# Attention and a channel MLP on one core: both heads of a pair read by one instruction where their PSUM banks lie side by side

## The chip, the core and the metric

The program runs on one core of one Trainium2 chip. A core has a matrix engine (TensorE, PE in the profile), a vector engine (VectorE, DVE), an engine for activation functions (ScalarE, ACT), a general engine (GpSimd, POOL) and a queue that issues most of the DMAs (SyncE, SP). TensorE writes its results into PSUM, which here is eight banks of 128 partitions by 512 float32; VectorE and ScalarE read them there. The metric is the device time of one execution in microseconds. The kernel before takes 2213.96 us (median of 3 runs, 2212.55 to 2215.34).

## What is computed

```python
def _A_ref(x, wqkv, wo):            # x: 1 x 2048 x 576
    H = 32; Dh = D // H             # 32 heads of 18
    qkv = (x @ wqkv).reshape(B, S, 3, H, Dh).transpose(2, 0, 3, 1, 4)
    q, k, v = qkv[0], qkv[1], qkv[2]
    p = softmax(einsum("bhqd,bhkd->bhqk", q, k) * Dh ** -0.5)
    o = einsum("bhqk,bhkd->bhqd", p, v)
    return o.transpose(0, 2, 1, 3).reshape(B, S, D) @ wo

def _B_ref(x, w1, b1, w2, b2):      # 576 -> 4608 -> 576
    h = gelu(einsum("bsd,df->bsf", layernorm(x), w1) + b1)
    return einsum("bsf,fd->bsd", h, w2) + b2

g = sigmoid((x * gate_w).sum(-1, keepdims=True))
out = g * _A_ref(x, wqkv, wo) + (1 - g) * _B_ref(x, w1, b1, w2, b2)
```

All of it is float32. Full attention over 2048 tokens with 32 heads of 18 and the MLP are independent of each other until the last line.

## The kernel before

Most matrix products take float32 operands split into a high and a low part, so that three fast products stand for one. A head has 18 columns; a query tile holds them three times (18 high, 18 high, 18 low) and a key tile to match, so one score matmul has 54 rows of depth. Heads are worked two at a time: head 0 of a pair lies on rows 0 to 63 of the array, head 1 on rows 64 to 127, and their two matmuls run side by side. Two such matmuls, one per head, are called a **pair** below.

The softmax takes two passes over the scores.

- **The maxima** (`s1_round`, L230 and L232). A pair of score matmuls, 128 queries by 512 keys for each head, goes into two banks, and VectorE reduces each bank to one maximum per query with `tensor_reduce`. This is called a max pair. After 32 rounds `s1_finish` puts the maxima into two extra rows of the query tile.
- **The exponentials** (`s2`, L275 and L278). A pair of score matmuls with 56 rows of depth (the maxima are in the product) gives 128 keys by 512 queries for each head, and ScalarE writes the exponential of each bank into a tile `p`. This is called an exp pair.
- **The product with V** (`pv`, L293). Two or three chunks of 128 keys at a time, their `p` tiles go through a burst of matmuls into one bank that collects the output of a unit (two heads, 1024 queries).

The program has 32 units of 16 chunks; a chunk has two half rounds. Each half round issues one exp pair of this unit and one max pair of a later unit (the maxima run ahead), so the two kinds alternate. 40 max pairs run before the loop, during the projection of Q, K and V. Between the pairs lie pieces of the MLP, cut to fill: `h_pair` (72 of them, 27 pairs of matmuls on 512 columns each, L494) and `out_pair` (144 of them, 24 pairs on 288 columns, L582). The readers of the MLP's banks are L514 on VectorE and L515 on ScalarE for the first, L599 on VectorE (two instructions) for the second; a Gelu chain in between goes over ScalarE and GpSimd (L547, L545, L183). The order on every engine is the order in which the code emits (`manual_schedule`); each engine takes its instructions in this order and waits at one until its semaphores are there. The weight load of a matmul is an instruction of its own (PEld in the profile), and a matmul's wait stands at its weight load.

**Banks.** A pool of PSUM tiles hands out its banks in turn, and the first matmul into a bank waits until the last reader of that bank is done. In the loop the scores have five banks, given out by `score_bank`: three of the pool `ps_s1` and then two of `ps_s2`, so bank after bank in a ring of five. A pair takes two places of the ring: the pair number k has places 2k and 2k+1, counted modulo 5. So the bank of a pair's head 0 was last used by head 1 of the pair three back, which is of the other kind, and the bank of head 1 was last used by head 0 of the pair two back, which is of the same kind. One bank holds the output of `pv` (`ps_o`), two are for the MLP (`ps_w`). Before the loop the scores have three banks and `ps_o`, and four more serve the projections.

Of the kernel before, what the change touches and what calls it, by code (L numbers as in the profile page):

```python
# [8 lines left out]
F32 = mybir.dt.float32  # L9
F32R = mybir.dt.float32r  # L10
AF = mybir.ActivationFunctionType
ALU = mybir.AluOpType
# [4 lines left out]
P = 128  # L17
# [16 lines left out]
GC0 = 1.0 / 0.044715  # L34
LN_EPS = 1e-5
HALF = S // 2
NS1 = 3
LEAD = 4
FILL = 1250.0
SLOT = 950.0  # L40
# [29 lines left out]
def gated_mix_kernel(ctx: ExitStack, tc: tile.TileContext, x, wqkv, wo, w1, b1, w2, b2, gate_w, out):  # L70
# [32 lines left out]
    pp = ctx.enter_context(tc.tile_pool(name="pp", bufs=2))  # L103
    hp = ctx.enter_context(tc.tile_pool(name="hp", bufs=6))
    asm = ctx.enter_context(tc.tile_pool(name="asm", bufs=2))
    ps_s1 = ctx.enter_context(tc.tile_pool(name="ps_s1", bufs=NS1, space=PSUM))
    ps_o = ctx.enter_context(tc.tile_pool(name="ps_o", bufs=1, space=PSUM))
    QA = [att.tile([P, HALF], F32R, name=f"qa{i}") for i in range(3)]
    KA = [att.tile([P, S], F32R, name=f"ka{i}") for i in range(2)]
    VT = [att.tile([P, NT, VW], F32, name=f"vt{i}") for i in range(2)]  # L110
# [2 lines left out]
    V0 = att.tile([P, NT, VW], F32, name="v0")  # L113
    oe = att.tile([P, TB], F32, name="oe")

    def psum(pool):
        return pool.tile([P, TB], F32, name="ps")

    ring = [0]

    def score_bank():

        ring[0] += 1
        if not looped[0]:
            return psum(ps_s1 if ring[0] % (NS1 + 1) < NS1 else ps_o)
        return psum(ps_s1 if ring[0] % (NS1 + 2) < NS1 else ps_s2)

    def big_tile():
        return yp.tile([P, 9, TB], F32R, name="big")
# [62 lines left out]
    def unit(u):  # L192
        return UNITS[u]
# [26 lines left out]
    def s1_round(u, r):  # L220


        t, kb = (r % 8, r // 8) if u in (0, NU - 3) else divmod(r, 4)
        if r == 0:
            M4[u] = asm.tile([P, 2, 8, 4], F32, name="m4")
        qa, ka = QA[u % 3], KA[unit(u)[0] % 2]
        for h in range(2):
            r0 = 64 * h
            ps = score_bank()
            nc.tensor.matmul(ps, qa[r0:r0 + 54, t * P:(t + 1) * P], ka[r0:r0 + 54, kb * TB:(kb + 1) * TB],  # L230
                             start=True, stop=True)
            nc.vector.tensor_reduce(M4[u][:, h, t, kb:kb + 1], ps, axis=AX.X, op=ALU.max)  # L232

    def s1_finish(u):

# [28 lines left out]
    def p_of(n):  # L264
        return RING[n % 4 if n < TWOS else (n - TWOS) % 3]

    def s2(u, kc, qb):
        qa, ka = QA[u % 3], KA[unit(u)[0] % 2]
        n = u * NT + kc
        if n < 2 and qb == 0:  # L270
            RING.insert(n, pp.tile([P, 2, 2, TB], F32, name="p"))
        ps = [score_bank() for _ in range(2)]
        for h in range(2):
            r0 = 64 * h
            nc.tensor.matmul(ps[h], ka[r0:r0 + 56, kc * P:(kc + 1) * P], qa[r0:r0 + 56, qb * TB:(qb + 1) * TB],  # L275
                             start=True, stop=True)
        for h in range(2):
            nc.scalar.activation(p_of(n)[:, qb, h], ps[h], AF.Exp, scale=SCALE)  # L278

    OB = {}  # L280

    def pv(n, m):

        u, kc = divmod(n, NT)
        if kc == 0:
            OB[u] = psum(ps_o)
        v = v_of(unit(u)[0])
        for c in range(n, n + m):
            for qb in range(2):
                for h in range(2):  # L290
                    r = 32 * (2 * h + qb)
                    k = c % NT
                    nc.tensor.matmul(OB[u][r:r + 32, :], v[:, k, 19 * h:19 * h + 32], p_of(c)[:, qb, h, :],  # L293
                                     start=(k == 0), stop=(k == NT - 1))
        if kc + m == NT:
            o_store(u, OB.pop(u))
# [45 lines left out]
    def mlp():  # L342
# [122 lines left out]
        def h_pair(q, last, inner=False):  # L465
# [5 lines left out]
                yield 0  # L471
            wt = ready(W1, q)
            del W1[q]
            ps = [psum(ps_w) for _ in range(2)]
# [77 lines left out]
        def out_pair(i, t, acc):  # L552

            tb, g = seq[i]
            tok = slice(t * P, (t + 1) * P)
            cs = [slice(nn * ND, (nn + 1) * ND) for nn in range(2)]
            ps = [psum(ps_w) for _ in range(2)]
            skip.clear()
            if piece[0]:
                ends = cuts(24, GAPS - piece[0]) | {12}  # L560
            elif rounds:
                ends = set(TURNS)
                skip.add(3)
            else:
                ends = set(TAIL)
                skip.update((2, 3))
            k = 0
            ends_at = []
            for turn in range(2):
                if turn == 1:  # L570
                    nc.tensor.wait_ge(swap, swaps[0])
                for j in ORDER:
                    while (i, j) not in HT:
                        cut[0] = 3
                        yield 0
                    hh, hl = HT[i, j]
                    w_ = ready(W2, (i * (G // 2) + j // 2, j % 2))
                    for h_, p_ in ((hh, 0), (hh, 1), (hl, 0)):
                        for h in (0, 1) if turn == 0 else (1, 0):
                            r = slice(64 * h, 64 * h + 64)  # L580
                            nn = h ^ turn
                            mm = nc.tensor.matmul(ps[nn][:, :ND], h_[r, tok], w_[p_][r, cs[nn]],  # L582
                                                  start=(k == 0), stop=(k == 6 * G - 1))
                            if k == 3 * G - 1:
                                ends_at.append(mm)
                        k += 1
                        if k == 3 * G:

                            seen = nc.scalar.sem_inc(swap, 1)
                            swaps[0] += 1  # L590
                            for mm in ends_at:
                                behind_of(seen, mm)
                        if k < 6 * G:
                            if k in ends:
                                cut[0] = 1
                            yield 131
            for nn in range(2):
                dst = acc[:, t, cs[nn]]
                nc.vector.scalar_tensor_tensor(dst, ps[nn][:, :ND], 0.5, b2b[:, cs[nn]] if g == 0 else dst,  # L599
                                               op0=ALU.mult, op1=ALU.add)  # L600
# [116 lines left out]
    with ExitStack() as a:  # L717
        wpool = a.enter_context(tc.tile_pool(name="a_w", bufs=1, side="right"))
        sm = a.enter_context(tc.tile_pool(name="a_sm", bufs=2, side="right"))
        ps_a = a.enter_context(tc.tile_pool(name="ps_a", bufs=4, space=PSUM))  # L720

        qkstack = ExitStack()
        wqk = qkstack.enter_context(tc.tile_pool(name="a_wqk", bufs=1))
# [41 lines left out]
                eng.tensor_tensor(lo[:, cs], raw[:, cs], hi[:, cs].bitcast(F32), op=ALU.subtract)  # L765

        def transposed(tb, c):
            ps = psum(ps_a)
# [66 lines left out]

        def stat_rows(tb):

            ps = psum(ps_a)
# [47 lines left out]
        def qk_group(tb, mt):  # L886
            big = xT[tb]
            wh, wl = W_QK
            ms = slice(mt * P, (mt + 1) * P)
            ps = psum(ps_a)  # L890
            k = 0
            for c in range(4):
                for w_, s_ in ((wh, c), (wh, 4 + c), (wl, c)):
# [12 lines left out]
        def v_group(tb, t, n, between=None):  # L906
# [4 lines left out]
            ps = psum(ps_a)  # L911
            k = 0
            for c in range(4):
                for s_, w_ in ((c, wh), (c, wl), (4 + c, wh)):
# [36 lines left out]
        for tb in range(NB):  # L951
            work = [(qk_group, (tb, mt)) for mt in (range(9) if tb < 2 else (4, 0, 1, 2, 3, 5, 6, 7, 8))] + [(v_group, (tb, t, n)) for t in range(4) for n in range(2)]
            for g, (fn, args) in enumerate(work):
# [35 lines left out]
                if tb == NB - 1:  # L989
                    if g == 0:  # L990
                        next(stream[0])
                    if g == 1:
                        load_k(0, 3 * TB, S)
                    if g == 2:
                        load_q(1)
                        next(stream[0])
                    if g == 9:
                        qkstack.close()
                        wp1 = mstack.enter_context(tc.tile_pool(name="m_w1", bufs=3))
                        wp2 = mstack.enter_context(tc.tile_pool(name="m_w2", bufs=4))  # L1000
                        next(stream[0])
                    if g == 7:
                        ps = psum(ps_a)
                        nc.tensor.transpose(ps[:, :NFC], b1r, ident[:NFC, :NFC])
                        nc.vector.tensor_copy(b1t, ps[:, :NFC])
                if tb == 1 and g == 5:
# [19 lines left out]
                    run_due()  # L1026


    ps_s2 = ctx.enter_context(tc.tile_pool(name="ps_s2", bufs=2, space=PSUM))
    ps_w = ctx.enter_context(tc.tile_pool(name="ps_w", bufs=2, space=PSUM))  # L1030
    cw = ctx.enter_context(tc.tile_pool(name="c_w", bufs=1, side="right"))
    ring2 = cw.tile([P, 2, 2, TB], F32, name="ring2")
    rstack = ExitStack()
# [7 lines left out]
    def out_proj():  # L1041
# [165 lines left out]
        for b in range(NB):  # L1207
# [6 lines left out]
            for t in range(4):  # L1214
# [5 lines left out]
                res = io.tile([P, D], F32, name="res", bufs=6)  # L1220
                for n in range(2):
                    cs = slice(n * ND, (n + 1) * ND)
                    ps = psum(ps_w)
                    k = 0
                    for c in range(5):
                        while done[b] <= c:
# [120 lines left out]
```

## Time and profile before

| | |
|---|---|
| median of 3 runs | 2213.96 us |
| profiled execution | 2212.78 us, of which the span of the instructions is 2211.0 us |
| TensorE busy | 2197.4 us (99%) |
| weight loads busy | 1578.5 us (71%) |
| VectorE busy | 1647.9 us (75%), 2888 instructions |
| ScalarE busy | 1425.9 us (64%), 2623 instructions |
| GpSimd busy | 1003.7 us (45%) |
| granted TensorE clock | 1.000 |

The times that follow are of the profiled execution. A busy TensorE is not one at its peak: the ends of matmuls are modelled, and a matmul that started late is not seen as idle time. A row of the groups gives the busy time (overlaps counted once), the mean length of one instruction, and behind the second bar the idle time of the engine before these instructions with what ended most of it. In the timeline a row is one or more like instructions in succession: start, length from the first start to the last end, engine, line, operation and count.

### The profile page before, as it was taken

The page shows a single profiled execution, that of the slowest core. Times are in us where ns is not written, and L with a number is a line of the kernel's source. Part 1 is how long each engine was busy: PE and PEld are TensorE (multiplying, and loading weights), DVE is VectorE, ACT ScalarE, POOL GpSimd, SP SyncE. Part 2 cuts the span into 40 slices and gives each one's busy share as a digit, 9 for nine tenths or more (in the row PEclk, how much of TensorE's full clock was granted, in tenths as well). Part 3 has the DMA queues.
Part 4 walks back from the last instruction along what each step waited for, and adds up shares of the span by engine and source line. Part 5 has one row for each costly group of instructions (what it writes and reads, how often), then busy time and mean ns, then how long its engine had stood idle before and what let it go on. Part 6 is the DMA issues. An engine that isn't in the chain of part 4 may idle for free.

```text
span 2211.0 us, 51479 instructions
## 1 busy us (share of the span) xinstructions
PE 2197.4 (99%) x20496; PEld 1578.5 (71%) x20496; DVE 1647.9 (75%) x2888; ACT 1425.9 (64%) x2623; POOL 1003.7 (45%) x1000
## 2 busy tenths in 40 slices
PE   8999999999999999999999999999999999999999
PEld 7877666676667776677766777767776777776668
DVE  6675777777778778777777777777776777777734
ACT  4333777777776666666666666666665666666672
POOL 4331766666664444444444444444444444444800
PEclk9999999999999999999999999999999999999999
DMA  8867655444464623333354424233464333242265
GB/s 263 276 217 224 199 175 156 154 160 151 152 198 139 197 101 123 121 124 105 115 173 150 138 81 136 101 125 101 125 176 146 109 113 120 98 153 101 77 224 169
DMA packets 171640, 329.74 MB, mean 149 GB/s; under 512 B 65314, under 2 KB 91614, under 8 KB 160672
## 3 DMA queue, kind: packets, MB, share of 16 engines
q1 hardware_dynamic: 168850, 322.67, 45.2%
q8 instruction: 161, 2.64, 0.5%
q10 hardware_dynamic: 2454, 3.75, 0.5%
q14 instruction: 79, 0.65, 0.1%
q0 software_dynamic: 96, 0.03, 0.0%
HBM read 234.00 MB, written 96.69 MB: 150 GB/s over the span
## 4 chain that ended last, share of the span: by engine, by line
PE 95%; DVE 2%; DMA 1%; issue 0%; POOL 0%; ACT 0%; SPq 0%; DVEq 0%; ACTq 0%; POOLq 0%
PE ps L293 21%; PE ps L582 21%; PE ps L494 20%; PE ps L275 13%; PE ps L230 11%; PE ps L894 3%; PE ps L1229 3%; PE ps L915 2%; DVE m L232 1%; PE ps L770 0%; DMA p<-in_A_wqkv_dram 0%; DMA big<-y_scr 0%; PE ps L897 0%; PE ps L896 0%; DVE st L857 0%
## 5 line engine op out<-in xcount | busy, mean ns | idle before, releaser
L232 DVE TENSOR_REDUCE m<-ps 128x1 f32<-128x512 f32 x2048 | 1311.3, 684 | 390.3 <-PE ps L230 380.3
L278 ACT ACTIVATE p<-ps 128x512 f32<-128x512 f32 x1048 | 568.3, 597 | 301.7 <-PE ps L275 299.3
L278 ACT ACTIVATE ring<-ps 128x512 f32<-128x512 f32 x1000 | 543.2, 596 | 294.9 <-PE ps L275 291.8
L494 PE MATMUL ps<-big,w 64*128 64x512 f32 x3708 | 569.4, 393 | 0.2 <-issue 0.2
L183 POOL TENSOR_SCALAR zz<-zz 128x512 f32<-128x512 f32 x288 | 178.1, 618 | 743.3 <-ACT zz L547 686.1
L582 PE MATMUL ps<-w,hh 64*128 64x288 f32 x4352 | 477.4, 294 | 1.5 <-DVE x L599 1.5
L275 PE MATMUL ps<-qa,ka 56*128 56x512 f32 x2048 | 448.6, 420 | 1.1 <-ACT p L278 0.3
L582 PEld LDWEIGHTS ps<-w,hh 64*128 64x128 f32 x4352 | 417.2, 186 | 32.5 <-DVE x L599 6.2
L230 PE MATMUL ps<-ka,qa 54*128 54x512 f32 x2048 | 425.6, 397 | 0.1
L494 PEld LDWEIGHTS ps<-big,w 64*128 64x128 f32 x3708 | 369.8, 187 | 66.1 <-issue 0.5
L183 POOL TENSOR_TENSOR zz<-zz,z 128x512 f32<-128x512 f32 x288 | 371.4, 1290 | 24.0
L275 PEld LDWEIGHTS ps<-qa,ka 56*128 56x128 f32 x2048 | 204.4, 184 | 226.3 <-DVE m L232 174.7
L582 PE MATMUL ps<-w,hl 64*128 64x288 f32 x2176 | 339.3, 292 | 0.8 <-POOL hl L183 0.8
L293 PE MATMUL ps<-p,vt 128*32 128x512 f32 x1968 | 239.1, 598 | 0.0
L230 PEld LDWEIGHTS ps<-ka,qa 54*128 54x128 f32 x2048 | 213.4, 184 | 22.6 <-DVE m L232 2.6
L293 PE MATMUL ps<-ring,vt 128*32 128x512 f32 x1872 | 227.6, 598 | 0.0
L582 PEld LDWEIGHTS ps<-w,hl 64*128 64x128 f32 x2176 | 222.2, 184 | 1.2 <-POOL hl L183 1.1
L183 POOL TENSOR_TENSOR hl<-zz,hh 128x512 fp32r<-128x512 f32 x136 | 176.6, 1299 | 11.4
L183 POOL TENSOR_TENSOR w<-x,w 128x576 fp32r<-128x576 f32 (+1 forms) x54 | 98.8, 1842 | 164.1 <-ACT w L398 158.4
L293 PEld LDWEIGHTS ps<-p,vt 128*32 128x32 f32 x1968 | 52.5, 109 | 111.8 <-issue 102.7
L293 PEld LDWEIGHTS ps<-ring,vt 128*32 128x32 f32 x1872 | 49.8, 109 | 106.4 <-issue 106.4
L599 DVE SCALAR_TENSOR_TENSOR x<-ps,x 128x288 f32<-128x288 f32 x256 | 103.6, 446 | 8.8 <-PE ps L582 8.4
(121 smaller groups left out, 1538.2 us busy)
## 6 DMA issues: line engine op xcount, KB each, us to landing
w<-w_scr SPq DMA_DIRECT2D x54, 1152.0 KB
w<-w_scr SPq DMA_DIRECT2D x108, 576.0 KB
x<-in_B_w_dram SPq DMA_DIRECT2D x72, 288.0 KB
w_scr<-w SPq DMA_DIRECT2D x18, 1152.0 KB
w_scr<-w SPq DMA_DIRECT2D x36, 576.0 KB
qa<-qk_scr SPq DMA_DIRECT2D x192, 72.0 KB
ka<-qk_scr SPq DMA_DIRECT2D x84, 144.0 KB
qk_scr<-hh SPq DMA_DIRECT2D x36, 256.0 KB
```

Of the source, the lines that this page charges most:

```text
L183: fn(*args, **kw)
L230: nc.tensor.matmul(ps, qa[r0:r0 + 54, t * P:(t + 1) * P], ka[r0:r0 + 54, kb * TB:(kb + 1) * TB], start=True, stop=True)
L232: nc.vector.tensor_reduce(M4[u][:, h, t, kb:kb + 1], ps, axis=AX.X, op=ALU.max)
L275: nc.tensor.matmul(ps[h], ka[r0:r0 + 56, kc * P:(kc + 1) * P], qa[r0:r0 + 56, qb * TB:(qb + 1) * TB], start=True, stop=True)
L278: nc.scalar.activation(p_of(n)[:, qb, h], ps[h], AF.Exp, scale=SCALE)
L293: nc.tensor.matmul(OB[u][r:r + 32, :], v[:, k, 19 * h:19 * h + 32], p_of(c)[:, qb, h, :], start=(k == 0), stop=(k == NT - 1))
L494: nc.tensor.matmul(ps[h], wt[w_][r, c, :], y[r, c, :], start=(k == 0), stop=(k == 26))
L582: mm = nc.tensor.matmul(ps[nn][:, :ND], h_[r, tok], w_[p_][r, cs[nn]], start=(k == 0), stop=(k == 6 * G - 1))
L599: nc.vector.scalar_tensor_tensor(dst, ps[nn][:, :ND], 0.5, b2b[:, cs[nn]] if g == 0 else dst, op0=ALU.mult, op1=ALU.add)
L894: nc.tensor.matmul(ps, w_[:, c, ms], big[:, s_, :], start=(k == 0), stop=False)
L915: nc.tensor.matmul(ps[:, :ND], big[:, s_, tok], w_[:, c, cs], start=(k == 0), stop=False)
L1229: nc.tensor.matmul(ps[:, :ND], OT[b][2][:, s_, tok], w_part(w_, c)[:, cs], start=(k == 0), stop=(k == 13))
```

## The change

All eight banks become one tile `PS`, and a table says which banks serve which use. The ring of five for the scores in the loop is banks 0 to 4 in this order, the same rotation as before. `score_banks` hands out a pair's two banks at once. Where the second is the next bank up, one access covers both, and the reader, `tensor_reduce` or the exponential, is issued once for both heads; where the pair is (4, 0), one pair in five, the two heads are read one after the other as before. Before the loop the scores have banks 0, 1, 2 and 5, where the pair (0, 1) is read at once and (2, 5) is not. Nothing else is computed in another way.

```diff
-    ps_s1 = ctx.enter_context(tc.tile_pool(name="ps_s1", bufs=NS1, space=PSUM))
-    ps_o = ctx.enter_context(tc.tile_pool(name="ps_o", bufs=1, space=PSUM))
+    PS = ctx.enter_context(tc.tile_pool(name="ps", bufs=1, space=PSUM)).tile([P, 8, TB], F32, name="ps")
...
-    def psum(pool):
-        return pool.tile([P, TB], F32, name="ps")
-
-    ring = [0]
-
-    def score_bank():
-
-        ring[0] += 1
-        if not looped[0]:
-            return psum(ps_s1 if ring[0] % (NS1 + 1) < NS1 else ps_o)
-        return psum(ps_s1 if ring[0] % (NS1 + 2) < NS1 else ps_s2)
+    BANKS = {"s": (0, 1, 2, 5), "a": (3, 4, 6, 7), "o": (5,), "w": (6, 7)}
+    given = {}
+
+    def bank(use):
+
+        given[use] = given.get(use, -1) + 1
+        return BANKS[use][given[use] % len(BANKS[use])]
+
+    def psum(use):
+        return PS[:, bank(use)]
+
+    def score_banks():
+
+        pair = (bank("s"), bank("s"))
+        if pair[1] == pair[0] + 1:
+            return [PS[:, b] for b in pair], [(slice(0, 2), PS[:, pair[0]:pair[1] + 1])]
+        return [PS[:, b] for b in pair], [(slice(h, h + 1), PS[:, b:b + 1]) for h, b in enumerate(pair)]
...
+        ps, reads = score_banks()
         for h in range(2):
             r0 = 64 * h
-            ps = score_bank()
-            nc.tensor.matmul(ps, qa[r0:r0 + 54, t * P:(t + 1) * P], ka[r0:r0 + 54, kb * TB:(kb + 1) * TB],
+            nc.tensor.matmul(ps[h], qa[r0:r0 + 54, t * P:(t + 1) * P], ka[r0:r0 + 54, kb * TB:(kb + 1) * TB],
                              start=True, stop=True)
-            nc.vector.tensor_reduce(M4[u][:, h, t, kb:kb + 1], ps, axis=AX.X, op=ALU.max)
+        for hs, banks in reads:
+            nc.vector.tensor_reduce(M4[u][:, hs, t, kb], banks, axis=AX.X, op=ALU.max)
...
-        ps = [score_bank() for _ in range(2)]
+        ps, reads = score_banks()
         for h in range(2):
             r0 = 64 * h
             nc.tensor.matmul(ps[h], ka[r0:r0 + 56, kc * P:(kc + 1) * P], qa[r0:r0 + 56, qb * TB:(qb + 1) * TB],
                              start=True, stop=True)
-        for h in range(2):
-            nc.scalar.activation(p_of(n)[:, qb, h], ps[h], AF.Exp, scale=SCALE)
+        for hs, banks in reads:
+            nc.scalar.activation(p_of(n)[:, qb, hs], banks, AF.Exp, scale=SCALE)
...
-    ps_s2 = ctx.enter_context(tc.tile_pool(name="ps_s2", bufs=2, space=PSUM))
-    ps_w = ctx.enter_context(tc.tile_pool(name="ps_w", bufs=2, space=PSUM))
+    BANKS["s"] = (0, 1, 2, 3, 4)
+    given["s"] = -1
```

In the built programs TensorE's instructions stand in the same order. What differs there is what the score matmuls wait for. The place is in the loop, in an `out_pair`; the names in brackets are the semaphores of the engines (`DVE_49` counts VectorE's instructions, `Activation_49` ScalarE's), and a matmul with no name of this kind waits for no reader. L275 before is L280 after, L230 is L234, L582 is L587. Before:

```order
L230 MATMUL ps<-ka_108,qa_106 128x512 [waits Activation_49]
L230 MATMUL ps<-ka_108,qa_106 128x512 [waits DVE_49]
L275 MATMUL ps<-qa_107,ka_109 128x512 [waits DVE_49]
L275 MATMUL ps<-qa_107,ka_109 128x512 [waits Activation_49]
L582 MATMUL ps<-w_13279,hh 128x288 [waits swap]
L582 MATMUL ps<-w_13279,hh 128x288 x3
```

After, at the same place:

```order
L234 MATMUL ps<-ka_106,qa_104 128x512 [waits Activation_49]
L234 MATMUL ps<-ka_106,qa_104 128x512 [waits DVE_49]
L280 MATMUL ps<-qa_105,ka_107 128x512
L280 MATMUL ps<-qa_105,ka_107 128x512 [waits Activation_49]
L587 MATMUL ps<-w_10831,hh 128x288 [waits swap]
L587 MATMUL ps<-w_10831,hh 128x288 x3
```

Head 0 of the exp pair no longer waits by itself; head 1 waits for ScalarE in both programs, before for the read of head 0 of the exp pair two back, now for the one read of both its heads.

On VectorE, between the two accumulations of an `out_pair` (L599 before, L604 after), the maxima stood one per head:

```order
L599 SCALAR_TENSOR_TENSOR x<-ps,x 128x288 [waits PE_49] x2
L232 TENSOR_REDUCE m_7843<-ps 128x1 [waits PE_49] x8
L599 SCALAR_TENSOR_TENSOR x<-ps,x 128x288 [waits PE_49] x2
L232 TENSOR_REDUCE m_7843<-ps 128x1 [waits PE_49] x2
L304 COPY oe<-ps 128x512 [waits DMAHW6_49,DMAHW5_49,DMAHW7_49,DMAHW0_49,PE_49]
```

and now stand so:

```order
L604 SCALAR_TENSOR_TENSOR x<-ps,x 128x288 [waits PE_49] x2
L237 TENSOR_REDUCE m_8055<-ps 128x1 [waits PE_49,Activation_49]
L237 TENSOR_REDUCE m_8055<-ps 128x1 [waits PE_49]
L237 TENSOR_REDUCE m_8055<-ps 128x2 [waits PE_49,Activation_49] x3
L604 SCALAR_TENSOR_TENSOR x<-ps,x 128x288 [waits PE_49] x2
```

A row with `128x2` reads both banks of a pair; the two rows with `128x1` are the pair (4, 0). The whole program has 1241 maximum instructions where it had 2048, and 1229 exponentials where it had 2048. The added wait for ScalarE is for the reader of the bank before, which the matmul had already waited for.

More of the change, by code (lines that the diff above doesn't have):

```diff
@@ L36 @@
 HALF = S // 2
-NS1 = 3
 LEAD = 4
@@ L285, in pv @@
         if kc == 0:
-            OB[u] = psum(ps_o)
+            OB[u] = psum("o")
         v = v_of(unit(u)[0])
@@ L473, in h_pair @@
             del W1[q]
-            ps = [psum(ps_w) for _ in range(2)]
+            ps = [psum("w") for _ in range(2)]
             if q == 0:
@@ L556, in out_pair @@
             cs = [slice(nn * ND, (nn + 1) * ND) for nn in range(2)]
-            ps = [psum(ps_w) for _ in range(2)]
+            ps = [psum("w") for _ in range(2)]
             skip.clear()
@@ L719, in gated_mix_kernel @@
         sm = a.enter_context(tc.tile_pool(name="a_sm", bufs=2, side="right"))
-        ps_a = a.enter_context(tc.tile_pool(name="ps_a", bufs=4, space=PSUM))
         qkstack = ExitStack()
@@ L767, in transposed @@
         def transposed(tb, c):
-            ps = psum(ps_a)
+            ps = psum("a")
             for t in range(4):
@@ L836, in stat_rows @@
         def stat_rows(tb):
-            ps = psum(ps_a)
+            ps = psum("a")
             nc.tensor.transpose(ps[:, :P], stp, ident)
@@ L889, in qk_group @@
             ms = slice(mt * P, (mt + 1) * P)
-            ps = psum(ps_a)
+            ps = psum("a")
             k = 0
@@ L910, in v_group @@
             wh, wl = W_V
-            ps = psum(ps_a)
+            ps = psum("a")
             k = 0
@@ L1002, in gated_mix_kernel @@
                     if g == 7:
-                        ps = psum(ps_a)
+                        ps = psum("a")
                         nc.tensor.transpose(ps[:, :NFC], b1r, ident[:NFC, :NFC])
@@ L1222, in out_proj @@
                     cs = slice(n * ND, (n + 1) * ND)
-                    ps = psum(ps_w)
+                    ps = psum("w")
                     k = 0
```

## Prediction

> **What bounds the kernel now.** I read the page first (busy time, chain), then the costliest groups, then one stretch of the loop in the timeline.
>
> ```profile
> PE 2197.4 (99%) x20496; PEld 1578.5 (71%) x20496; DVE 1647.9 (75%) x2888; ACT 1425.9 (64%) x2623; POOL 1003.7 (45%) x1000
> PE 95%; DVE 2%; DMA 1%; issue 0%; POOL 0%; ACT 0%; SPq 0%; DVEq 0%; ACTq 0%; POOLq 0%
> ```
>
> TensorE is the bound: 95% of the chain that ended last, and it has 2211.0 - 2197.4 = 13.6 us of idle time in all. So nothing that VectorE or ScalarE saves can count by itself. It counts only through the moment at which a bank comes free.
>
> ```profile
> L232 DVE TENSOR_REDUCE m<-ps 128x1 f32<-128x512 f32 x2048 | 1311.3, 684 | 390.3 <-PE ps L230 380.3
> L278 ACT ACTIVATE p<-ps 128x512 f32<-128x512 f32 x1048 | 568.3, 597 | 301.7 <-PE ps L275 299.3
> L275 PE MATMUL ps<-qa,ka 56*128 56x512 f32 x2048 | 448.6, 420 | 1.1 <-ACT p L278 0.3
> L230 PE MATMUL ps<-ka,qa 54*128 54x512 f32 x2048 | 425.6, 397 | 0.1
> L230 PEld LDWEIGHTS ps<-ka,qa 54*128 54x128 f32 x2048 | 213.4, 184 | 22.6 <-DVE m L232 2.6
> ```
>
> TensorE sat idle 1.2 us before all its 4096 score matmuls. VectorE and ScalarE do wait for TensorE (380 us before L232, 299 before one half of L278), so as an average they have room. The change is decided by the order within a stretch between two bursts of `pv`:
>
> ```profile
> 1003.25 0.51 PE L275 MATMUL ps<-qa,ka 56*128 56x512 f32 x2
> ...
> 1003.99 0.41 PE L230 MATMUL ps<-ka,qa 54*128 54x512 f32 x2
> ...
> 1004.61 0.41 PE L275 MATMUL ps<-qa,ka 56*128 56x512 f32 x2
> ...
> 1005.64 0.42 PE L230 MATMUL ps<-ka,qa 54*128 54x512 f32 x2
> 1005.89 0.41 PE L275 MATMUL ps<-qa,ka 56*128 56x512 f32 x2
> ...
> 1006.92 0.41 PE L230 MATMUL ps<-ka,qa 54*128 54x512 f32 x2
> ...
> 1007.56 0.40 PE L275 MATMUL ps<-qa,ka 56*128 56x512 f32 x2
> ...
> 1008.19 0.41 PE L230 MATMUL ps<-ka,qa 54*128 54x512 f32 x2
> 1008.53 1.92 PE L293 MATMUL ps<-p,vt 128*32 128x512 f32 x16
> 1010.39 0.49 PE L275 MATMUL ps<-qa,ka 56*128 56x512 f32 x2
> ```
>
> Four pairs of each kind lie close together (the rows left out are `out_pair`, L582), then a burst of 1.9 us lets the readers catch up. From one max pair to the next it is 1.65, 1.28 and 1.27 us; from one exp pair to the next 1.36, 1.28 and 1.67.
>
> **The wait that the change lengthens.** The bank of a pair's head 1 was last used by head 0 of the same kind's pair before (two back). So far that bank is free once the first of the two readers is done; now only when the one reader has read both banks. Head 1's weight load waits for it, and everything on TensorE stands behind that load in order. The time from the start of a pair to the earliest start of head 1 in the next of its kind comes from these rows:
>
> ```profile
> 1006.08 0.69 DVE L232 TENSOR_REDUCE m<-ps 128x1 f32<-128x512 f32 x1 [0.38 <-PE ps L230]
> 1006.79 0.21 PEld L230 LDWEIGHTS ps<-ka,qa 54*128 54x128 f32 x2
> 1005.04 1.09 ACT L278 ACTIVATE p<-ps 128x512 f32<-128x512 f32 x2 [0.17 <-PE ps L275]
> 1006.08 1.29 DVE L232 TENSOR_REDUCE m<-ps 128x1 f32<-128x512 f32 x2 [0.38 <-PE ps L230]
> ```
>
> - Matmul start to reader start: max pair 1005.64 to 1006.08, exp pair 1004.61 to 1005.04: 0.43 us, mostly the matmul's own 0.40.
> - Reader end to matmul: the first maximum ends at 1006.08 + 0.69 = 1006.77. Of the two weight loads in the row at 1006.79, of 0.184 us each, the second ends at 1007.00, so it began at 1006.82, 0.05 after that end; its matmul is the second of the row at 1006.92, 0.11 after its load. Together 0.16 us. This load was already waiting for its bank, and the matmul was just in time. So the room is used up here before any change.
> - The reader of two banks is not in the trace. Its bounds: not under one single read (0.68 for the maximum, 0.60 for the exponential), not over two in succession, which overlap a little (1.29 and 1.09, the rows above). Between them I go by what more elements cost:
>
> ```profile
> L239 DVE TENSOR_REDUCE nm<-m 128x16 f32<-128x64 f32 x32 | 7.0, 220 | 1.1
> L922 ACT ACTIVATE vt<-ps 128x288 f32<-128x288 f32 x16 | 6.7, 417 | 20.8 <-PE ps L918 19.5 <-issue 1.0
> ```
>
> (684 - 220) / (512 - 64) = 1.04 ns an element on VectorE, so 0.68 + 512 x 1.04 ns = 1.21 us. (597 - 417) / (512 - 288) = 0.80 ns on ScalarE, so 0.60 + 0.41 = 1.01 us. Joining saves only 0.08 us a pair on either engine, and it holds head 0's bank 0.53 and 0.41 us longer.
>
> The least distance from pair to next pair of its kind is then 0.43 + 1.21 + 0.16 = 1.80 us for maxima (0.43 + 0.68 + 0.16 = 1.27 before) and 0.43 + 1.01 + 0.16 = 1.60 us for exponentials (1.19 before). The distances of 1.27 and 1.28 in the stretch were just met; they no longer are.
>
> **One stretch replayed.** Every delay moves all that follows on TensorE. Start from 1003.25 and 1003.99. The exp pair at 1004.61 cannot come before 1003.25 + 1.60 = 1004.85: 0.24 late. The max pair of 1005.64 comes at 1005.88, allowed from 1005.79. The exp pair of 1005.89, now 1006.13, is allowed from 1006.45: 0.32 more, 0.56 in all. The max pair of 1006.92, now 1007.48, is allowed from 1007.68: 0.20 more, 0.76. The exp pair of 1007.56 comes at 1008.32, allowed from 1008.05. The max pair of 1008.19, now 1008.95, is allowed from 1009.48: 0.53 more, **1.29 us** in all. The burst follows, so nothing of it is regained. One pair in five is (4, 0), read head by head, and its follower is free after 1.27 or 1.19 us as before. Over the five places where it can fall the delay is 1.29 three times and about 1.1 and 0.7 once each: mean 1.13 us. There are 144 `out_pair`, each about one such stretch (288 L599 instructions, two each): 144 x 1.13 = 163 us.
>
> A stretch with an `h_pair` is looser:
>
> ```profile
> 1414.79 0.40 PE L230 MATMUL ps<-ka,qa 54*128 54x512 f32 x2
> ...
> 1422.95 0.44 PE L230 MATMUL ps<-ka,qa 54*128 54x512 f32 x2
> ```
>
> These are the first and the last of six max pairs between two bursts, five distances of (1422.95 - 1414.79) / 5 = 1.63 us, and the exp pairs between them lie as far apart. Each distance of the maxima is 0.17 short, 0.85 over five, of which one is free for the split pair; the exp pairs are covered by the same delay: 0.7 us. 72 `h_pair` make 50 us.
>
> **The sum.** 163 + 50 = 213. Two things lower it. Head 0 of a held pair is let in first and can run ahead of head 1 by up to one pair (0.25 us, 1005.64 to 1005.89), until the burst needs both. And the maxima run ahead by 40 pairs, so the last stretches have none. I take 200 us. What else the change touches is nothing on TensorE: its instructions and their order are the same, the added waits are for readers that the matmul has already waited for, the 40 max pairs before the loop come at most two at a time between the matmuls of the projections. The ends of head 1's banks move 0.08 earlier, which relieves the exp pair that follows a max pair at once (1005.89 after 1005.64); it was in time already. 2212.8 + 200 = **2413 us**; the profiled execution is 1 us under the median of the runs, which I leave out.
>
> **The range.** With the reader at its upper bound (1.29 and 1.09) the distances are 1.88 and 1.68; the same replay gives 1.5 us and about 1.0: with the same allowance for the split pair (1.13 / 1.29 = 0.88), 0.88 x 1.5 x 144 + 72 = 262 us, 2475. With the lower bound (0.68 and 0.60) nothing is delayed: 2213. I hold the lower bound unlikely, since both engines' rows grow with their elements. Range 2335 to 2470.
>
> **Rivals.**
>
> 1. *Relief instead of delay (not slower).* Place: the weight loads of the exp pairs.
>
> ```profile
> PEld ps L275 <- DVE m L232: 174.7, 212, 0.8
> PEld ps L275 <- DVE x L599: 10.9, 13, 0.8
> PEld ps L275 <- issue: 8.5, 11, 0.8
> ```
>
> If these 212 waits for the maxima were time that TensorE loses, each would shrink by the 0.08 us that joining saves: 212 x 0.08 = 17 us, 2196. It decides if no bank is asked for before a joined reader is done, that is, if pairs of a kind lay over 1.8 us apart. Against it: the waits are 0.82 us each whoever is named, also for "issue" (8.5 / 11 = 0.77), so this is the pause of the weight loads within a `pv` burst and no wait; and the distances above are under 1.8. The Trainium skill, Advanced Engine Details and Errata, section The Read-Write Bubble, takes this side: it counts a bubble between instructions of ScalarE and VectorE and advises large tiles and reading several PSUM banks with one instruction. The trace agrees that there is something to save (0.08 us a pair by my estimate), but not that TensorE waits for it. Chance 5%.
>
> 2. *The second bank is cheap, or half the delay is covered.* If the second 512 elements cost half (0.94 and 0.80 us), the distances are 1.53 and 1.39: then the stretch at 1003 loses about 0.5 us and the one at 1414 none: 144 x 0.5 = 72, 2285. Against it the slopes of two engines. Chance 8%.
>
> 3. *The clock.* More pauses on TensorE might cost granted clock. If it fell to 0.9 on average, 2197 us of matmuls would take 244 more, on top of the 200: 2657. Against it:
>
> ```profile
> 3.00:6.00 3.00, 1.15 (x6) 1.18 (x7) 0.00 (x0) 0.03 (x1) 2.85 (x6) 1.00 1.08 378
> ```
>
> TensorE was busy 1.15 of these 3 us, and the clock is 1.00; the pauses to come are at most 0.5 us each. The Trainium skill, TensorE: Matmul & The Clock Gate, section A second HAM failure mode: psum-queue depth-cycling, tells of short idle times between groups of matmuls that cycle through banks, with the clock going down and up. No row here shows it. Chance 3%.
>
> 4. *One tile, one wait.* If the single tile made each matmul wait for every read of it, 2000 pairs would cost 1.8 us each, over 3 ms. The order shows it isn't so: head 0 of most pairs waits for no reader. Chance 1%.
>
> **Chances.** The forecast has 83%. Two times of this kernel can be told apart from about 0.2%, some 4 us. Faster by more: 4%, all of rival 1; within 0.2%: 2%, what is left of it and a reader near its lower bound; slower: 94%.
>
> **What would show it.** Right: a joined maximum near 1.21 us and a joined exponential near 1.01; VectorE's and ScalarE's busy time down by some 60 us each; more idle time before L230 and L275 or their weight loads, named for the maxima and exponentials; in a stretch like the one at 1003, distances of at least 1.8 and 1.6 except after a split pair; `pv` bursts and the time before the loop unchanged. Wrong: joined readers well under these, distances still 1.27 with no wait, or a clock under 1.00.

## The result, and the profile after

The changed kernel takes 2475.24 us (median; 2474.44 to 2475.88), the kernel before beside it 2214.65 us (2212.55 to 2216.07): a ratio of 1.1177 with a 95% interval of [1.1158, 1.1197], 261 us slower. The forecast was 2413 us with a range up to 2470. Direction and place are as foretold; the size is not: 261 us where 200 were forecast, and 5 us over the range.

Busy time and chain of the changed kernel:

```profile
span 2474.1 us, 51216 instructions
PE 2395.4 (97%) x20496; PEld 1592.1 (64%) x20496; DVE 1605.0 (65%) x2081; ACT 1381.8 (56%) x1804; POOL 1002.9 (41%) x1000
PE 79%; DVE 12%; ACT 4%; DMA 2%; issue 2%; SPq 0%; DVEq 0%; POOL 0%; ACTq 0%
```

VectorE's busy time fell by 43 us and ScalarE's by 44, with 1600 instructions fewer between them. Yet 12% and 4% of the chain that ended last now run over these two engines, where it was 2% and 0%. The groups by form (a mean then belongs to one shape):

```profile
L237 DVE TENSOR_REDUCE m<-ps 128x2 f32<-128x1024 f32 x807 | 988.2, 1225 | 568.5 <-PE ps L234 483.5 <-PE ps L280 42.3 <-ACT ring L283 18.2
L283 ACT ACTIVATE p<-ps 128x1024 f32<-128x1024 f32 x420 | 430.0, 1025 | 380.9 <-PE ps L280 352.0 <-PE ps L587 14.1 <-DVE m L237 11.0
```

The joined reader takes 1.225 us on VectorE and 1.025 us on ScalarE (estimated: 1.21 and 1.01). And now TensorE waits by name (waits: in total, times, longest):

```profile
PEld ps L234 <- DVE m L237: 203.2, 452, 1.0
```

That is the weight loads of the max pairs, for which 2.6 us stood in the trace before. The stretch that the prediction replayed, 1003.25 to 1010.39, now runs from 1110.54 to 1119.27 (counted by exp pairs from the start of the loop): 8.73 us where it was 7.14, so 1.59 more. Shown are its first exp pair and then all pairs of the stretch behind it, which is of the same form:

```profile
1110.54 0.50 PE L280 MATMUL ps<-qa,ka 56*128 56x512 f32 x2
...
1119.27 0.50 PE L280 MATMUL ps<-qa,ka 56*128 56x512 f32 x2
1120.00 0.40 PE L234 MATMUL ps<-ka,qa 54*128 54x512 f32 x2
1120.64 0.77 PE L280 MATMUL ps<-qa,ka 56*128 56x512 f32 x2
1121.81 0.40 PE L234 MATMUL ps<-ka,qa 54*128 54x512 f32 x1
1122.05 0.40 PE L234 MATMUL ps<-ka,qa 54*128 54x512 f32 x1
1122.05 0.97 PE L280 MATMUL ps<-qa,ka 56*128 56x512 f32 x2
1123.42 0.40 PE L234 MATMUL ps<-ka,qa 54*128 54x512 f32 x1
1123.83 0.49 PE L234 MATMUL ps<-ka,qa 54*128 54x512 f32 x1
1124.34 0.39 PE L280 MATMUL ps<-qa,ka 56*128 56x512 f32 x1
1124.57 0.39 PE L280 MATMUL ps<-qa,ka 56*128 56x512 f32 x1
1124.97 0.39 PE L234 MATMUL ps<-ka,qa 54*128 54x512 f32 x1
1125.71 0.49 PE L234 MATMUL ps<-ka,qa 54*128 54x512 f32 x1 [0.35 <-DVE m L237]
1126.13 1.92 PE L298 MATMUL ps<-ring,vt 128*32 128x512 f32 x16
1127.98 0.50 PE L280 MATMUL ps<-qa,ka 56*128 56x512 f32 x2
```

Before the change this second stretch began at 1010.39, and the exp pair after its burst was this:

```profile
1017.52 0.50 PE L275 MATMUL ps<-qa,ka 56*128 56x512 f32 x2
```

Pairs that were one row of two matmuls have come apart: head 0 goes at 1123.42 and head 1 at 1123.83, at 1124.97 and 1125.71. From the first exp pair to the one after the burst it is 1127.98 - 1119.27 = 8.71 us, where it was 1017.52 - 1010.39 = 7.13: 1.58 us more. Head 1 of the last two max pairs starts at 1123.83 and 1125.71, a distance of 1.88. The links of that distance:

```profile
1122.55 1.23 DVE L237 TENSOR_REDUCE m<-ps 128x2 f32<-128x1024 f32 x1 [0.76 <-PE ps L280]
1124.43 1.23 DVE L237 TENSOR_REDUCE m<-ps 128x2 f32<-128x1024 f32 x1 [0.65 <-PE ps L234]
```

```profile
1123.83 0.18 PEld L234 LDWEIGHTS ps<-ka,qa 54*128 54x128 f32 x1 [0.25 <-DVE m L237]
1125.71 0.18 PEld L234 LDWEIGHTS ps<-ka,qa 54*128 54x128 f32 x1 [0.59 <-DVE m L237]
```

The reader ends at 1122.55 + 1.23 = 1123.78; 0.05 us later head 1's weight load starts, and its matmul with it. The matmul takes 0.49 instead of 0.40: its weight load starts with it, where the load at 1006.79 in the trace before came 0.13 us ahead of its matmul. It ends at 1124.32; the reader starts at 1124.43, 0.11 us later; it runs 1.23 and ends at 1125.66, and at 1125.71 the next load starts. 0.05 + 0.49 + 0.11 + 1.23 = 1.88 us. The prediction had 1.80. Its 0.43 + 0.16 for matmul and release came to 0.05 + 0.49 + 0.04 = 0.58 plus something new: the reader starts 0.11 us after the matmul's end where it was 0.04 (a single reader before starts at 1006.08, its matmul of 1005.64 ends 0.40 us on). What stands there shows in the list of VectorE's line:

```profile
L237 DVEq EVENT_SEMAPHORE  x983: 21/21/21, 220.7 to 2358.2; - x197
```

These are waits with an instruction of their own ahead of the maximum. The kernel before has one on this line. The order shows why: `[waits PE_49,Activation_49]` is two waits, and in the trace the one for TensorE stands in the EVENT_SEMAPHORE, the one for ScalarE in the maximum behind it. The exponential that the second wait asks for had ended at least 0.96 us before the matmul's end in all 983 cases. Where the prediction counted this wait at nothing because it has long been satisfied, it still stands between the matmul's end and the reader.

### The profile page after: what moved, and what is told of

It reads as the page before. It is cut to its first block, busy times and chain, and to the rows that moved or that the text cites. A ratio compares the mean times of both kernels' runs of the same rounds, so it can differ in the third digit from the quotient of the medians.

```text
span 2474.1 us, 51216 instructions
## 1 busy us (share of the span) xinstructions
PE 2395.4 (97%) x20496; PEld 1592.1 (64%) x20496; DVE 1605.0 (65%) x2081; ACT 1381.8 (56%) x1804; POOL 1002.9 (41%) x1000
## 4 chain that ended last, share of the span: by engine, by line
PE 79%; DVE 12%; ACT 4%; DMA 2%; issue 2%; SPq 0%; DVEq 0%; POOL 0%; ACTq 0%
PE ps L298 19%; PE ps L499 16%; PE ps L234 15%; PE ps L280 13%; PE ps L587 11%; DVE m L237 11%; PE ps L898 3%; PE ps L1233 2%; ACT ring L283 2%; ACT p L283 2%; PE ps L919 1%; DMA p<-in_A_wqkv_dram 0%; DMA bt<-b_scr 0%; DMA mx_scr<-tr 0%; DMA x<-in_A_x_dram 0%
## 5 line engine op out<-in xcount | busy, mean ns | idle before, releaser
L237 DVE TENSOR_REDUCE m<-ps 128x2 f32<-128x1024 f32 (+1 forms) x1241 | 1264.9, 1036 | 674.0 <-PE ps L234 574.9
L283 ACT ACTIVATE p<-ps 128x1024 f32<-128x1024 f32 (+1 forms) x628 | 543.4, 883 | 453.9 <-PE ps L280 423.4
L283 ACT ACTIVATE ring<-ps 128x1024 f32<-128x1024 f32 (+1 forms) x601 | 519.4, 881 | 447.9 <-PE ps L280 423.3
L234 PE MATMUL ps<-ka,qa 54*128 54x512 f32 x2048 | 671.3, 419 | 60.2 <-DVE m L237 59.0
L280 PE MATMUL ps<-qa,ka 56*128 56x512 f32 x2048 | 628.5, 434 | 6.9 <-ACT p L283 1.1
L587 PE MATMUL ps<-w,hh 64*128 64x288 f32 x4352 | 599.1, 300 | 0.9 <-DVE x L604 0.9
L280 PEld LDWEIGHTS ps<-qa,ka 56*128 56x128 f32 x2048 | 309.6, 184 | 306.6 <-issue 163.8
L587 PEld LDWEIGHTS ps<-w,hh 64*128 64x128 f32 x4352 | 476.0, 186 | 18.2 <-DVE x L604 2.7
L234 PEld LDWEIGHTS ps<-ka,qa 54*128 54x128 f32 x2048 | 317.2, 184 | 221.1 <-DVE m L237 203.2
L587 PE MATMUL ps<-w,hl 64*128 64x288 f32 x2176 | 453.0, 292 | 0.0
L587 PEld LDWEIGHTS ps<-w,hl 64*128 64x128 f32 x2176 | 330.2, 185 | 0.1
L604 DVE SCALAR_TENSOR_TENSOR x<-ps,x 128x288 f32<-128x288 f32 x256 | 103.7, 446 | 19.9 <-PE ps L587 14.1
```

What stands on the lines that cost most here:

```text
L234: nc.tensor.matmul(ps[h], qa[r0:r0 + 54, t * P:(t + 1) * P], ka[r0:r0 + 54, kb * TB:(kb + 1) * TB], start=True, stop=True)
L237: nc.vector.tensor_reduce(M4[u][:, hs, t, kb], banks, axis=AX.X, op=ALU.max)
L283: nc.scalar.activation(p_of(n)[:, qb, hs], banks, AF.Exp, scale=SCALE)
```

## The experiments

Theory: the loss is the time for which head 0's bank is held, set by the least distance between two pairs of a kind (matmul, reader, release, with 0.07 us for the added wait). Rivals: the one tile, the joined form of the instruction, one of the two engines alone. The numbers of the theory come from the trace of before: all pairs of the loop are put down at their start, and each is moved back until the least distance to the pair of its kind before it is kept; everything behind moves with it. For the changed kernel itself this gives 208 us with 1.80 and 1.60, and 250 us with 1.88 and 1.61, of the measured 261. How the replay treats pairs that already lay closer than the least distance shifts these sums: with such pairs left as much closer as they were they are 213 and 251 us, with every pair held to the full distance 227 and 265. The step between the two pairs of distances stays at 38 to 42 us. All runs are compared with runs of the kernel before beside them, 2213 us.

**One tile, every bank read on its own.**

```diff
-    def score_banks():
+    def score_banks(joined=True):
...
-        if pair[1] == pair[0] + 1:
+        if joined and pair[1] == pair[0] + 1:
...
-        ps, reads = score_banks()          # in s1_round and in s2
+        ps, reads = score_banks(False)
```

> The change's one tile and its table of banks, but every bank read by an instruction of its own, head 0 first, as before. Theory (the loss comes from head 0's bank being held until both heads are read, plus a wait that stands ahead of a joined maximum): the least distances are 1.27 us for maxima and 1.19 for exponentials again, as before, and no place of the loop is held: 2213 us, plus or minus 8. Rival (one tile for all banks brings waits that cost by themselves): most of the 261 us of the change stay, above 2400 us.

Measured: 2215.17 us, ratio 1.001 [1.000, 1.002]. The tile and the table of banks cost at most some 0.2%. VectorE's line of the maxima shows 72 waits with an instruction of their own, not 983. Where VectorE was idle before, the reads behind them start 0.107 us after their matmul's end (median of 71), those without such a wait 0.038 us (533), though every read here covers one bank.

**Head 1 read first, nothing joined.**

```diff
-        return [PS[:, b] for b in pair], [(slice(h, h + 1), PS[:, b:b + 1]) for h, b in enumerate(pair)]
+        return [PS[:, b] for b in pair], [(slice(h, h + 1), PS[:, b:b + 1]) for h, b in reversed(list(enumerate(pair)))]
```

on top of the run above.

> As the run with one tile and split reads, but of the two reads of a pair that of head 1 comes first and that of head 0 second. No instruction covers two banks. Theory: head 0's bank comes free after both reads, 1.29 us (maxima) and 1.09 us (exponentials) after the reader's start, and here for every pair, also where the banks do not lie side by side. Least distances 0.43 + 1.29 + 0.16 = 1.88 us and 0.43 + 1.09 + 0.16 = 1.68 us; the distances of the trace of before, replayed with these, give 296 us: 2510 us, between 2470 and 2540. Rival (a single instruction over two banks is what costs, by its form or by both engines reading across banks): no such instruction here, so about 2214 us.

Measured: 2526.76 us, ratio 1.1417 [1.1400, 1.1434], 313 us slower. No instruction is joined, both engines do the work of the kernel before, and the loss is larger than that of the change. Its chain and groups:

```profile
PE 77%; DVE 12%; ACT 6%; issue 3%; DMA 2%; POOL 0%; SPq 0%; ACTq 0%; DVEq 0%
L237 DVE TENSOR_REDUCE m<-ps 128x1 f32<-128x512 f32 x2048 | 1315.6, 685 | 690.1 <-PE ps L234 626.2
L234 PE MATMUL ps<-ka,qa 54*128 54x512 f32 x2048 | 682.5, 422 | 56.7 <-DVE m L237 51.4
```

The reads are the 2048 short ones of before (685 ns), VectorE is idle 690 us before them, and TensorE waits for them. So it is not the instruction's form but the moment at which head 0's bank is let go.

**The maxima joined alone, and the exponentials joined alone.**

```diff
-        ps, reads = score_banks()          # in s1_round, in s2
+        ps, reads = score_banks(True)      # joined in one of the two
+        ps, reads = score_banks(False)     # head by head in the other
```

> The change with the maxima of both heads joined and the exponentials one per head. Theory: distances of maxima 0.05 + 0.50 + 0.11 + 1.23 = 1.88 us as the trace after shows them, of exponentials 1.19; replayed on the trace of before this gives 232 us: 2446 us, between 2410 and 2465, so nearly the whole loss, because the delays of the two kinds cover one another. If the added wait ahead of the joined maximum cost nothing, the distance would be 1.81 and the replay gives 190 us: 2404. Rival (ScalarE's joined reads cause the loss): about 2214 us.

> The change with the exponentials of both heads joined and the maxima one per head. Theory: distance of exponentials 1.61 us, of maxima 1.27 to 1.34; the replay gives 84 to 94 us: 2303 us, between 2280 and 2320. Together with the run that joins the maxima alone this would be more than the whole (232 + 89 = 321 against 261). Rival (the two losses simply add up): 2214 + 261 less what the other run shows, some 2240 us.

Measured: maxima 2441.13 us, ratio 1.1031 [1.1014, 1.1047], 228 us; exponentials 2314.39 us, ratio 1.0456 [1.0440, 1.0471], 101 us. Replayed: 232 and 84 to 94. Together 329 us where the change itself loses 261: a stretch that has been drawn out for the maxima leaves room for the exponentials. The maxima alone are most of it; their least distance is the longer one (1.88 against 1.61 us). In the run with the exponentials joined 802 of the single maxima carry the added wait too, which is why the replay gave two numbers for it. 228 is also the first sign that the added wait has its price, for without it the replay gave 190.

**Four banks, no second wait.**

```diff
-    BANKS["s"] = (0, 1, 2, 3, 4)
+    BANKS["s"] = (0, 1, 2, 3)
```

> The change with banks 0 to 3 alone for the scores in the loop, bank 4 left unused: exp pairs always take (0, 1), max pairs always (2, 3), so every read is joined, both heads of a pair wait for the pair before of their kind, and no bank goes from one engine's reads to the other's. The built order shows no wait for ScalarE at a joined maximum any more. Theory that this added wait costs 0.07 us each time (matmul end to reader 0.107 us in the trace after, 0.037 before): distance of maxima 0.05 + 0.50 + 0.04 + 1.23 = 1.82 us, of exponentials 1.61; the replay, with no split pairs, gives 251 us: 2465 us, 2455 to 2485 with what the replay was short in the earlier runs (up to 17 us), so no slower than the change itself though every pair is joined and one bank is gone. Rival (the added wait costs nothing, and the maximum's distance of 1.88 has another cause): the replay with 1.88 for every pair gives 289 us: 2502 us, up to 2520.

Measured: 2488.33 us, ratio 1.1243 [1.1224, 1.1261], 275 us. This lies between the two: 3 us over the theory's range, 14 under the rival's number. By the time alone it settles nothing; here both heads of a pair wait at once, and head 0 cannot go ahead. Nor is ScalarE free of a second wait: where it was idle before, 457 exponentials with a wait instruction ahead start 0.102 us after the matmul's end and 517 without at 0.042 (medians), and the theory's 1.61 us left that out. The trace does show the reader's start without the second wait, at a held max pair:

```profile
1135.88 0.50 PE L234 MATMUL ps<-ka,qa 54*128 54x512 f32 x2
```

```profile
1136.42 1.23 DVE L237 TENSOR_REDUCE m<-ps 128x2 f32<-128x1024 f32 x1 [0.60 <-PE ps L234]
```

Matmul end 1136.38, reader 1136.42: 0.04 us.

**The same with the second wait put back.**

```diff
-            nc.vector.tensor_reduce(M4[u][:, hs, t, kb], banks, axis=AX.X, op=ALU.max)
+            mx = nc.vector.tensor_reduce(M4[u][:, hs, t, kb], banks, axis=AX.X, op=ALU.max)
+            if len(exps) > 1:              # exps: the exponentials issued so far
+                tc.add_manual_dep(mx.ins, exps[-2].ins.name, mybir.DependencyInfo(
+                    mybir.DependencyClass.Sync, mybir.DependencyReason.DATA), reason="added wait")
...
-            nc.scalar.activation(p_of(n)[:, qb, hs], banks, AF.Exp, scale=SCALE)
+            exps.append(nc.scalar.activation(p_of(n)[:, qb, hs], banks, AF.Exp, scale=SCALE))
```

on top of the run above.

> The run with four banks, and one thing added: each joined maximum in the loop also waits for the exponential of the exp pair before last, which has long been done, so that the built order shows the wait for ScalarE beside that for TensorE again. Nothing else differs. Theory (such a second wait, though already satisfied, puts the reader's start off by 0.07 us): matmul end to reader 0.107 us again, distance of maxima 1.82 + 0.07 = 1.89 us; the replay goes from 251 to 289 us, 38 more: 2488 + 38 = 2526 us, between 2510 and 2540. Rival (a satisfied wait costs nothing): 2488 us, within 5.

Measured: 2525.46 us, ratio 1.1407 [1.1388, 1.1426]. 37 us more than without it, where 38 were expected. Its list of VectorE's line and a held pair:

```profile
L238 DVEq EVENT_SEMAPHORE  x983: 21/21/21, 221.3 to 2407.0; - x197
```

```profile
1134.80 0.50 PE L235 MATMUL ps<-ka,qa 54*128 54x512 f32 x2
```

```profile
1135.41 1.23 DVE L238 TENSOR_REDUCE m<-ps 128x2 f32<-128x1024 f32 x1 [0.67 <-PE ps L235]
```

Matmul end 1135.30, reader 1135.41: 0.11 us again. The second wait makes 983 instructions, as many as in the changed kernel, and the exponential that it asks for had ended at least 1.24 us before the matmul's end each time. ScalarE's waits are those of the run before (458 reads at 0.102 us, 519 at 0.042). So a satisfied wait, put ahead of a reader that TensorE waits for, costs 0.07 us at such a place, and 37 us in this kernel.

**Half the columns, maxima joined.**

```diff
-            nc.vector.tensor_reduce(M4[u][:, hs, t, kb], banks, axis=AX.X, op=ALU.max)
+            nc.vector.tensor_reduce(M4[u][:, hs, t, kb], banks[:, :, :TB // 2], axis=AX.X, op=ALU.max)
```

on top of the run with the maxima joined alone.

> The run with joined maxima and split exponentials, but each maximum reads only the first 256 of the 512 columns of a bank, so half of the scores are left out of the maxima; a joined read is then 512 elements, about 0.69 us. Banks, instructions, waits and their order are the same. Theory (the length of the read that holds head 0's bank sets the loss): distance of maxima 0.05 + 0.50 + 0.11 + 0.69 = 1.35 us against 1.27; the replay gives 21 us: 2234 us, between 2215 and 2245. Rival (the joined form itself, a read across two banks, slows TensorE): 2441 us as with the full read, or at least above 2350.

Measured: 2225.77 us, ratio 1.0058 [1.0043, 1.0073]. The instructions are joined, their waits and their order are those of the run with the maxima joined, of which the first row is; only the reads are shorter, as the second row shows (means over joined and single reads):

```profile
L237 DVE TENSOR_REDUCE m<-ps 128x2 f32<-128x1024 f32 (+1 forms) x1241 | 1265.3, 1036 | 640.9 <-PE ps L234 541.8
```

```profile
L237 DVE TENSOR_REDUCE m<-ps 128x2 f32<-128x512 f32 (+1 forms) x1241 | 719.4, 596 | 872.0 <-PE ps L234 714.6
```

Of the 228 us of the loss 215 are gone, with the joined form, the tile and the added waits all still there.

**Half the columns, every bank on its own.** The same edit on top of the run with one tile and split reads.

> One tile, every bank read on its own, head 0 first, and each maximum reads only the first 256 of 512 columns (half of the scores are left out of the maxima). VectorE's reads of the scores are thus some 0.27 us shorter and its busy time some 550 us less. Theory (TensorE is the bound and the readers of before are just in time): nothing to be won by faster readers, 2205 to 2216 us. Rival (TensorE lost time to the maxima in the kernel before, so that relief of VectorE would pay): 2195 us or less.

Measured: 2204.96 us, ratio 0.9962 [0.9949, 0.9975], 8 us faster and at the lower edge of what was expected.

```profile
PE 2188.8 (99%) x20496; PEld 1571.3 (71%) x20496; DVE 1121.4 (51%) x2888; ACT 1424.2 (65%) x2623; POOL 1003.9 (46%) x1000
```

With a third of VectorE's work taken away (1121 us busy where it was 1648) TensorE gains 0.4%. That bounds what a relief of VectorE at the maxima could have brought. The difference to the joined run with the same half reads, 2225.77 - 2204.96 = 21 us, is what the replay gave for distances of 1.35 us. No run beats the kernel before with all its work done.

## Why the prediction was wrong, point by point

**What bounds the kernel** was right: TensorE, with readers that are just in time. The last run shows it from the other side.

**The lengthened wait** was right in its place (head 1's weight load, two pairs back, same kind), and so was the fall of the distances under the least one. The reversed order of reads gives an even larger loss (313 us) without any joined instruction, and half the read takes 215 us off the 228 of the joined maxima.

**The durations** were right: 1.21 and 1.01 us estimated, 1.225 and 1.025 measured. The saving of 0.08 us a pair is 0.07 against two reads in succession. The busy time of the two engines fell by 43 and 44 us, where some 60 each were foretold.

**The step that failed** is "the added waits are for readers that the matmul has already waited for", by which they were costed at nothing. The matmul had waited for them, but the wait is a further instruction on VectorE, 0.07 us between the matmul's end and the reader, on the very loop that sets the distance. It makes the least distance of the maxima 1.88 us, not 1.80; replayed, 38 to 42 us more. Put in alone, in the four-bank kernel, it cost 37. So it is some 40 of the 61 us by which the forecast was short; 13 more are the reduction below.

The price stood in the trace of before, on the other engine. ScalarE's line there has 482 such waits:

```profile
L278 ACTq EVENT_SEMAPHORE  x482: 17/17/17, 220.7 to 2159.0; - x161
```

Most of them hold the wait for TensorE and leave a second one, for ScalarE's own count, to the exponential behind. Where ScalarE was idle before, these reads of head 0 start 0.098 us after the end of their matmul (median of 412), the ones without such a wait 0.038 us (496). After the change the line has still more of them:

```profile
L283 ACTq EVENT_SEMAPHORE  x928: 17/17/17, 215.7 to 2423.7; - x186
```

But now 909 have the two waits the other way round: the satisfied one, for VectorE, stands ahead, and the exponential itself waits for TensorE. Joined reads behind these start 0.037 us after the matmul's end (median of 652), and the distance of the exponentials is 1.61 us where 1.60 was estimated. So it is the order of the two waits that decides.

**The reduction** from 213 to 200 was wrong too, as to its first reason. Head 0 does go ahead (1123.42 before 1123.83), but the loss shows nothing regained: the replay without any allowance for it gives 250 us (251 or 265 in the other two ways) of the measured 261. It is not exact enough to say where the last few us come from, and no run tried it. The second reason held: the four `out_pair` stretches behind the last maxima lose nothing.

**By stretch:** the one at 1003 was to lose 1.29 us and lost 1.59. 144 such stretches were to lose 163 us, at 1.13 on average; the 140 that still have maxima lost 188, at 1.34. The stretches with an `h_pair` were to lose 50 and lost 74. What lies before and behind the loop gave 1.3 us more. The one with an `h_pair` at 1411 was to lose 0.7; here are its bursts before and after:

```profile
1411.28 1.92 PE L293 MATMUL ps<-ring,vt 128*32 128x512 f32 x16
...
1423.31 1.07 PE L293 MATMUL ps<-p,vt 128*32 128x512 f32 x8
```

```profile
1579.68 1.92 PE L298 MATMUL ps<-ring,vt 128*32 128x512 f32 x16
...
1592.73 1.06 PE L298 MATMUL ps<-p,vt 128*32 128x512 f32 x8
```

13.05 us from burst to burst against 12.03 before, so 1.02. With the distance at 1.88 instead of 1.80, five distances of 1.63 are each 0.25 short instead of 0.17.

**Rivals.** Relief fell: 8 us is all that a third less work on VectorE brings. The cheap second bank fell with the durations. The clock fell as a rival, with 0.999 over the run, but it did go down once. Behind two idle times of TensorE of 0.68 and 0.76 us, at 1896.37 and 1898.25, it was at 0.50 for 3.4 us, and a burst of 16 matmuls that takes 1.92 us elsewhere took 3.62. The prediction had reckoned with pauses of 0.5 us at most. In these rows the number behind the stretch is its length, the next one TensorE's busy time, and the third from the end the granted clock:

```profile
1895.30:1898.70 3.40, 1.96 (x17) 1.13 (x18) 2.24 (x2) 2.49 (x4) 2.79 (x3) 1.00 0.76 242
1898.70:1902.10 3.40, 3.40 (x17) 0.57 (x16) 1.23 (x1) 0.00 (x0) 3.08 (x4) 0.50 0.71 252
```

```profile
1898.67 3.62 PE L298 MATMUL ps<-p,vt 128*32 128x512 f32 x16
```

This is 1.7 us of the 261. The four other runs that lose over 200 us show one such drop each, of 3.4 to 6.8 us; the kernel before and the other runs show none in the loop. It is the only place of this run that fits what the Trainium skill tells of short idle times between groups of matmuls (TensorE: Matmul & The Clock Gate, section A second HAM failure mode: psum-queue depth-cycling); the clock does not go down and up again, with TensorE 97% busy. "One tile, one wait" fell: 2215 us with one tile and split reads. The 2475 us that the prediction worked out for a reader at its upper bound came out almost to the number, by luck: the readers took 1.225 and 1.025 us, not 1.29 and 1.09, and the maxima came to its distance of 1.88 us through the added wait. The stated range ended at 2470, 5 us below that bound of its own.

## What to carry to other kernels

Joining two reads of PSUM saves one instruction's overhead (here 0.07 us) and holds the first bank until the second is read (here 0.54 us longer); before joining, ask which matmul takes the first bank next, and how soon. Add up the loop matmul, reader, release, and compare it with the least distance in the tightest stretch, not with the average load of the engine. And count every wait that the tool puts ahead of an instruction on this loop, also one that is always satisfied, and look at which of two waits stands last.

## What was not expected of the hardware

- A second, satisfied wait on VectorE cost 0.07 us per instruction when the wait for TensorE stood in the instruction ahead: 0.107 us from the matmul's end to the reader against 0.037, and 37 us in the whole kernel when it was put in alone. With the satisfied wait ahead and the one for TensorE in the reader itself, ScalarE started at 0.037 us.
- A matmul whose weight load was held back runs 0.50 us instead of 0.40, its weight load starting with it; together with 0.05 us from the reader's end to the load this is the cost of a bank that comes late.
- The order of two reads alone, head 1 before head 0, made the kernel 14% slower with the same matmuls and reads on every engine, though by then the replay had given 2510 us for it.
- The granted clock went to 0.50 for 3.4 us with no idle time of TensorE over 0.76 us near it.
